# Making the second copy of v by DMA within SBUF instead of on GpSimd, in a windowed-attention and gated-layers kernel

## The chip, the cores and the metric

The kernel runs on one core of one Trainium2 chip. The metric is the device time of one execution in microseconds (us). A core has TensorE (matrix products, and weight loads beside them), VectorE (DVE in the profile), ScalarE (ACT), GpSimd (POOL) and SyncE (SP), which here does nothing but issue DMAs; 16 DMA engines move the data.

## What is computed

Three parts follow one another, all in float32:

```python
# q, k, v: (4, 8, 576, 64); a query sees itself and the 63 keys before it
scores = scale * q @ k.T                 # masked outside 0 <= i - j < 64
attn = softmax(scores)
x = (attn @ v)  reshaped to 2304 x 512
x = (silu(x @ w_gate) * (x @ w_val)) @ w_out      # 512 -> 1536 -> 512
y = ((x @ w1) * (x @ w2)) @ w3 @ w_out2           # 512 -> 1024 -> 512
```

The weights come as float64 and are read as pairs of 32-bit words.

## The kernel before

**Attention.** Two heads of one batch form a unit; there are 4 x 4 = 16 units, each cut into three sub-blocks of three 64-query windows. One iteration `m` treats two sub-blocks, so there are `NM` = 24 iterations, and the loop runs three more to drain its pipeline. In iteration `m` TensorE computes the scores of `m` (L400, L410) into PSUM, transposes raw q and k of later units (T, L373), computes the products with v of iteration `m - 3` (PV, L463) and transposes the probabilities of `m - 2` (PT, L443). VectorE takes the maxima (L417), the reciprocals of the sums (L430, L431), and evicts the transposed probabilities to SBUF (`ptt`, L449); ScalarE does the exponentials (L424) and copies the results to X (L477, L480); GpSimd multiplies the probabilities by the reciprocals (`pexp`, L434).

**The two copies of v.** A window of 64 queries needs 128 keys, that is two halves of 64. `load_v(u)` (L354, L356) loads v of unit `u` with its rows in blocks of 128. Windows that begin in the middle of a block need the halves paired the other way: the lower half of one tile from the upper part of the next block. `pair_v(u)` makes this second tile, `vt[u][1]`, by two copies on GpSimd (L362, L363), one for partitions 0 to 63 and one for 64 to 127, each 64 x 512 numbers (2 KB a partition). Units `u0` and `u0 + 1` are paired in the second and third iteration of their group of three; PV reads the copy two iterations later.

**The order.** Every engine's instructions run in the order in which the program emits them. In an iteration the loads of later units are emitted first, on SyncE: q and k (L347) four DMAs a unit, v three. `pair_v` stands behind the normalisation and ahead of `events(m, NM)`, which calls `during_attention`. There the helper work is placed: splitting the weights of the gate layer and the operands X into a high and a low part (casts L197, subtractions L201, sums L205; `narrow`, L185 to L191, turns float64 words into float32). A planner keeps a free time for each engine. `plan.charge(e, cost)` tells it what attention itself takes of an engine in this iteration; `plan.advance(3.85)` then places queued jobs on whichever of their engines can start first, as long as that start lies within the 3.85 us. Casts go to ScalarE or GpSimd, subtractions and sums to VectorE or GpSimd, the steps of `narrow` to VectorE and ScalarE alone. A job that needs a tile also needs a free slot: of 56 slots, 26 are kept for attention until it ends, and `slots` counts the others. After attention `plan.shut.add("POOL")` takes GpSimd out of the planner.

The 1 MB weight loads ("stage" loads, `st_...`, L227) go through SyncE as well. There are two buffers for them: from the third on, a stage load waits until the jobs on an earlier one are done, and SyncE issues nothing in the meantime.

**The gate.** Behind attention (and from its last three iterations on) `gated` computes the products with the weights (L578) from the split operands `xo`; from there on TensorE works without attention's interplay.

Of the kernel before, what the change touches and what calls it, by code (L numbers as in the profile page):

```python
# [32 lines left out]
def window_attention_moe_kernel(ctx: ExitStack, tc: tile.TileContext, q, k, v, w_gate, w_val, w_out, w1, w2, w3, w_out2, out):  # L33
    nc = tc.nc
# [26 lines left out]
    def slot(shape, dtype, name, counted=True):  # L61

        plan.slots -= counted
        return sl.tile(shape, dtype, tag="s", name=name)
# [266 lines left out]
    def attention(events):  # L331
        if True:
# [7 lines left out]
            raw, vt, qT, kT, sc, pexp, ptp, ptt, stat = {}, {}, {}, {}, {}, {}, {}, {}, {}  # L340
# [18 lines left out]
            def pair_v(u):  # L359

                t = slot([P, 4, 2, D], F32, f"v{u}_1", False)
                nc.gpsimd.tensor_copy(out=t[:64], in_=vt[u][0][:64, 1:])  # L362
                nc.gpsimd.tensor_copy(out=t[64:], in_=vt[u][0][64:, :4])  # L363
                vt[u].append(t)

            tbank = {}
# [146 lines left out]
            for m in range(NM + 3):  # L513
# [30 lines left out]
                for u in ((), (u0,), (u0 + 1,))[r]:  # L544
                    if u < U:
                        pair_v(u)
# [373 lines left out]
    def loads(n):  # L920
        while at[0] < min(n, len(coming)):
            coming[at[0]].load()
            at[0] += 1

    def make_to(x, rank=None):

        while at[1] <= coming.index(x):
            plan.rank = rank if rank is not None else 1 if isinstance(coming[at[1]], Weights) else 2
            loads(at[1] + 1)
            coming[at[1]].make()  # L930
            at[1] += 1
            loads(at[1] + 2)
            plan.rank = 0
# [74 lines left out]
    def during_attention(m, NM):  # L1008
        if m in (1, 3):
            loads(1 + m // 2)  # L1010
        if m == 3:
            make_to(left1[0, 1], 0)
        for tp, first in enumerate((13, 20, NM + 2)):
            if m == first:
                xop1[tp] = Operands([X[tp, c] for c in range(KC)], f"xo{tp}")
        if m < NM:
            for e, cost in (("DVE", 2.9), ("ACT", 3.2), ("POOL", 2.6)):
                plan.charge(e, cost)
            plan.advance(3.85)
        else:  # L1020
            for e, cost in (("DVE", (1.6, 1.1, 1.1)), ("ACT", (2.2, 0.5, 0.5)), ("POOL", (1.9, 0.0, 0.0))):
                plan.charge(e, cost[m - NM])
            for _ in range((3, 2, 2)[m - NM]):
                next(gate)

    with tc.manual_schedule():
        attention(during_attention)
        ident2 = own.tile([P, P], F32, name="ident2")
        nc.gpsimd.memset(ident2, 1.0)
        nc.gpsimd.affine_select(out=ident2, in_=ident2, pattern=[[-1, P]], compare_op=ALU.is_equal, fill=0.0,  # L1030
                                base=0, channel_multiplier=1)
        plan.shut.add("POOL")
        plan.slots += ATTENTION
        plan.ahead = 1.0
        for _ in gate:
            pass
        for _ in project(rows, wos, events_p):
            pass
        on(events2, len(order2) - 6, lambda: make_to(w3s[-1]))
        begin_e, run_e = final(rows2, ident2)  # L1040

        def put_all():
            for j in by:
                plan.need(j)
            begin_e()
        on(events2, len(order2) - 4, put_all)
        for _ in gated(xop2, left2, order2, AF.Copy, h2d, events2):
            pass
        run_e()
# [30 lines left out]
```

## Time and profile before

| | us |
|---|---|
| median of three runs | 873.38 |
| lowest and highest of them | 871.74, 873.64 |
| span of the profiled execution, first to last instruction | 869.7 |

The profiled execution's total is not among the times; its span is 3.7 us below the median. All times in the rows are counted from the span's start. A group of instructions reads: line, engine, operation, output<-inputs, shape, count | busy time in us, mean ns of one | idle time of the engine before them and what ended it.

### The profile page before, as it was taken

How to read it: one execution, taken by the hardware profiler on the slowest of the kernel's cores; microseconds unless marked ns; L12 is line 12 of the kernel's file. 1: busy time of each engine (PE TensorE's matmuls, PEld its weight loads, DVE VectorE, ACT ScalarE, POOL GpSimd, SP SyncE). 2: the span in 40 equal slices, each digit the busy share in tenths (PEclk: the TensorE clock that was granted, in tenths of full speed). 3: DMA queues.
4: the chain of work that ended last, by engine and by line, in shares of the span. 5: the costliest groups of instructions: out<-in, count | busy, mean ns of one | idle time of the engine just before them, and what ended most of it. 6: DMA issues, size and time to landing. Idle time of an engine off the chain costs nothing.

```text
span 869.7 us, 14819 instructions
## 1 busy us (share of the span) xinstructions
PE 839.7 (97%) x5610; PEld 791.1 (91%) x5610; DVE 582.2 (67%) x1173; ACT 421.2 (48%) x1075; POOL 86.2 (10%) x119
## 2 busy tenths in 40 slices
PE   7899888899999999999989999999999999999998
PEld 6777687899999999999989999999999998888886
DVE  4899958878688768875797573867788644531400
ACT  6878855464646454733465442445454423430300
POOL 3678930000000000000000000000000000000000
PEclk9999999999999999999999999999999999999999
DMA  9979300135356323599987331023545179131511
GB/s 198 218 159 188 93 1 37 40 126 189 111 186 219 124 104 151 200 350 402 369 300 245 119 122 49 37 71 123 194 158 193 50 267 362 39 131 64 179 49 48
DMA packets 112535, 136.23 MB, mean 157 GB/s; under 512 B 61392, under 2 KB 78032, under 8 KB 111440
## 3 DMA queue, kind: packets, MB, share of 16 engines
q1 hardware_dynamic: 112320, 135.16, 47.6%
q8 instruction: 44, 0.72, 0.4%
q14 instruction: 27, 0.22, 0.1%
q10 hardware_dynamic: 144, 0.13, 0.0%
HBM read 92.27 MB, written 42.99 MB: 156 GB/s over the span
## 4 chain that ended last, share of the span: by engine, by line
PE 81%; DVE 7%; DMA 5%; ACT 2%; SPq 2%; issue 1%; POOL 1%; POOLq 0%; ACTq 0%; DVEq 0%
PE ala L578 14%; PE alb L578 14%; PE o L707 12%; PE out L818 11%; PE beb L578 7%; PE bea L578 7%; PE acc L774 5%; PE gab L578 3%; PE gaa L578 3%; DMA wo<-wo 2%; DMA zd<-by_z 2%; PE PV L463 1%; DVE ptt L449 1%; SPq L347 1%; DMA st_z<-in_moe_w_out_dram 1%
## 5 line engine op out<-in xcount | busy, mean ns | idle before, releaser
L707 PE MATMUL o<-ph,wo 128*128 128x384 f32 x576 | 147.7, 337 | 2.7 <-ACT X L721 2.7
L707 PEld LDWEIGHTS o<-ph,wo 128*128 128x128 f32 x576 | 105.0, 189 | 3.0 <-ACT X L721 3.0
L707 PE MATMUL o<-pl,wo 128*128 128x384 f32 x288 | 96.9, 336 | 0.0
L585 ACT COPY ha<-ala 128x384 f32<-128x384 f32 x90 | 42.9, 479 | 51.5 <-PE ala L578 50.3
L589 DVE TENSOR_TENSOR ha<-ha,bea 128x384 f32<-128x384 f32 x60 | 33.2, 553 | 45.0 <-PE bea L578 26.6
L707 PEld LDWEIGHTS o<-pl,wo 128*128 128x128 f32 x288 | 54.5, 189 | 0.0
L424 ACT ACTIVATE pexp<-S,stat 128x128 f32<-128x128 f32 x144 | 51.8, 392 | 0.0
L599 ACT ACTIVATE ha<-ha 128x384 f32<-128x384 f32 x54 | 28.4, 526 | 39.0 <-DVE ha L589 39.0
L434 POOL TENSOR_TENSOR pexp<-pexp,stat 128x384 f32<-128x384 f32 x48 | 44.4, 945 | 28.5 <-DVE stat L431 22.6
L836 DVE COPY o<-out 128x512 f32<-128x512 f32 x11 | 7.6, 692 | 57.7 <-PE out L818 57.7
L201 DVE TENSOR_TENSOR pl<-pl,ph 128x768 fp32r<-128x768 f32 x36 | 33.5, 956 | 16.5 <-ACT ph L197 16.1
L197 ACT CAST ph<-pl 128x768 fp32r<-128x768 f32 x36 | 29.3, 835 | 31.1 <-DMA pl<-h 24.1
L585 ACT COPY c12b<-alb 128x384 f32<-128x384 f32 x30 | 14.5, 482 | 48.7 <-PE alb L578 48.6
L833 ACT COPY o<-out 128x512 f32<-128x512 f32 x6 | 3.5, 588 | 65.5 <-PE out L818 65.5
L589 DVE TENSOR_TENSOR c22b<-c22b,beb 128x384 f32<-128x384 f32 x30 | 16.6, 554 | 26.4 <-ACT c22b L585 26.3
L424 ACT ACTIVATION_READ_ACCUMULATOR pexp<-S,stat 128x1 f32 x144 | 33.1, 230 | 0.0
L417 DVE TENSOR_REDUCE stat<-S 128x3 f32<-128x384 f32 x48 | 24.3, 546 | 8.2 <-PE S L410 8.0
L463 PEld LDWEIGHTS PV<-ptt,v 128*64 128x64 f32 x576 | 19.5, 137 | 10.2 <-DVE ptt L449 5.7
L463 PE MATMUL PV<-ptt,v 128*64 128x64 f32 x576 | 22.9, 227 | 6.1 <-DVE ptt L449 5.0
L578 PE MATMUL ala<-xo,w_g_1h 128*128 128x384 f32 x120 | 26.9, 337 | 1.7 <-ACT w_g_1h L197 1.7
L201 DVE TENSOR_TENSOR xo<-X,xo 128x384 fp32r<-128x384 f32 x37 | 22.6, 641 | 5.7 <-ACT xo L197 5.7
L201 DVE TENSOR_TENSOR fl<-fl,fh 128x768 fp32r<-128x768 f32 x24 | 21.7, 952 | 6.9 <-ACT fh L197 6.9
(490 smaller groups left out, 2407.4 us busy)
## 6 DMA issues: line engine op xcount, KB each, us to landing
h<-ha SPq DMA_DIRECT2D x60, 384.0 KB, 3.2
pl<-h SPq DMA_DIRECT2D x36, 384.0 KB, 6.7
fl<-h SPq DMA_DIRECT2D x24, 384.0 KB, 6.1
st_w<-in_moe_w_dram SPq DMA_DIRECT2D x8, 1024.0 KB, 6.9
st_g<-in_moe_w_gate_dram SPq DMA_DIRECT2D x6, 1024.0 KB, 5.5
st_v<-in_moe_w_val_dram SPq DMA_DIRECT2D x6, 1024.0 KB, 5.4
st_wo<-in_moe_w_out_dram SPq DMA_DIRECT2D x6, 1024.0 KB, 5.8
wo<-by_wo SPq DMA_DIRECT2D x12, 512.0 KB, 3.9
```

What stands on the lines that cost most here:

```text
L197: (eng.copy if eng is nc.scalar else eng.tensor_copy)(out=hi(), in_=src())
L201: return plan.job(lambda eng: eng.tensor_tensor(out=lo(), in0=src(), in1=hi().bitcast(F32), op=ALU.subtract), after, slots=slots, DVE=dve( ...
L424: nc.scalar.activation(out=pe[:, jj, :], in_=so[:, jj, :], func=AF.Exp, bias=st[:, 0, x, jj:jj + 1], accum_out=st[:, 1, x, jj:jj + 1])
L434: nc.gpsimd.tensor_tensor(out=pe, in0=pe, in1=st[:, 3, x, :].unsqueeze(2).to_broadcast([P, SUB, P]), op=ALU.mult)
L463: nc.tensor.matmul(pp[64 * h:64 * h + 64, 64 * (SUB * x + jj):64 * (SUB * x + jj) + 64], lhsT=vt[u][e][:, at, h, :], rhs=t[:, x, jj, c:c + ...
L578: nc.tensor.matmul(acc, lhsT=self.wt.ops[p, x][:, m, :], rhs=self.xs.ops[p, m][:, y, :], start=start and n == 0, stop=n == 5, skip_group_c ...
L585: nc.scalar.copy(out=out, in_=src)
L589: nc.vector.tensor_tensor(out=out, in0=x, in1=y, op=ALU.add)
L599: nc.scalar.activation(out=h, in_=src, func=func)
L707: nc.tensor.matmul(acc[m, x], lhsT=wos.tiles[i // 6][:, i % 6, :], rhs=rows[2 * tp + x].words(f, b), start=f == n == 0, stop=f == NF - 1 a ...
L774: nc.tensor.matmul(acc, lhsT=w3T[i][c // 3][:, x, (c % 3) * P:(c % 3) * P + P], rhs=zt[c, y], start=c == n == 0, stop=c == NI - 1 and n == 2)
L818: nc.tensor.matmul(acc, lhsT=rows[blk].words(i, x)[:, t * P:t * P + P], rhs=w34[i][y], start=i == n == 0, stop=i == NI - 1 and n == 2)
```

## The change

`pair_v` issues two DMAs on SyncE, SBUF to SBUF, where it had two GpSimd copies, and GpSimd's charge for an iteration is lowered from 2.6 to 1.9 us. Nothing else changes.

```diff
             def pair_v(u):
 
                 t = slot([P, 4, 2, D], F32, f"v{u}_1", False)
-                nc.gpsimd.tensor_copy(out=t[:64], in_=vt[u][0][:64, 1:])
-                nc.gpsimd.tensor_copy(out=t[64:], in_=vt[u][0][64:, :4])
+                nc.sync.dma_start(out=t[:64], in_=vt[u][0][:64, 1:])
+                nc.sync.dma_start(out=t[64:], in_=vt[u][0][64:, :4])
                 vt[u].append(t)
...
         if m < NM:
-            for e, cost in (("DVE", 2.9), ("ACT", 3.2), ("POOL", 2.6)):
+            for e, cost in (("DVE", 2.9), ("ACT", 3.2), ("POOL", 1.9)):
                 plan.charge(e, cost)
             plan.advance(3.85)
```

## Rows read from the trace of the kernel before

**Rows 1.** The head of the page

```profile
span 869.7 us, 14819 instructions
PE 839.7 (97%) x5610; PEld 791.1 (91%) x5610; DVE 582.2 (67%) x1173; ACT 421.2 (48%) x1075; POOL 86.2 (10%) x119
```

**Rows 2.** Windows: stretch, its length, busy us of each engine (x instructions), clock, DMA

```profile
40.00:105.00 65.00, 58.07 (x968) 47.43 (x966) 60.93 (x130) 54.08 (x251) 54.71 (x71) 0.97 0.69 153
```

**Rows 3.** Waits of TensorE, 17 to 110 us: total us, times, longest

```profile
PE PV L463 <- DVE ptt L449: 4.8, 7, 1.5
PE T L373 <- DMA rawq<-in_q_dram: 1.8, 2, 1.5
PE T L373 <- DVE ptt L449: 1.4, 3, 0.6
```

**Rows 4.** Groups of VectorE, 40 to 105 us (22 two-input jobs in all)

```profile
L449 DVE COPY ptt<-PT 128x384 f32<-128x384 f32 x32 | 16.2, 544 | 0.0
...
L201 DVE TENSOR_TENSOR xo<-X,xo 128x384 fp32r<-128x384 f32 x5 | 5.7, 1151 | 0.0
...
L430 DVE TENSOR_SCALAR stat<-stat 128x6 f32<-128x6 f32 x15 | 3.0, 200 | 0.6 <-ACT pexp L424 0.6
...
L201 DVE TENSOR_TENSOR w_g_6h<-st_g,w_g_6h 128x256 fp32r<-128x256 f32 x1 | 0.4, 384 | 0.0
```

**Rows 5.** DMA, 0 to 40 us, in slices of 1 us: busy tenths, GB/s

```profile
DMA  0099999999999999936899999999999999969999
GB/s 0 14 224 219 229 220 226 214 200 186 214 203 201 211 199 208 211 73 66 301 399 357 268 213 213 213 214 220 197 328 406 336 253 209 199 124 221 227 235 211
```

**Rows 6.** Loads of v, 0 to 60 us: ns of one issue, min/median/max

```profile
L354 SPq DMA_DIRECT2D v<-in_v_dram x18: 468/542/1407, 5.3 to 49.3; - x18
```

**Rows 7.** Groups of GpSimd, whole span

```profile
L434 POOL TENSOR_TENSOR pexp<-pexp,stat 128x384 f32<-128x384 f32 x48 | 44.4, 945 | 28.5 <-DVE stat L431 22.6 <-ACT X L480 3.7 <-PE PV L463 1.4
L363 POOL COPY v<-v 64x512 f32<-64x512 f32 x16 | 10.2, 640 | 0.9
L362 POOL COPY v<-v 64x512 f32<-64x512 f32 x16 | 10.2, 636 | 0.0
```

**Rows 8.** Chain of waits, 76 to 110 us: start, us, what

```profile
103.63 1.14 POOL pexp L434
104.77 0.56 POOL v L362
...
105.38 0.62 POOL v L363
...
106.07 0.26 POOL X L205
...
107.02 1.62 POOL pexp L434 x2
```

**Rows 9.** Groups of VectorE, 160 to 200 us

```profile
L201 DVE TENSOR_TENSOR w_g_6l<-st_g,w_g_5l 128x256 fp32r<-128x256 f32 x2 | 0.8, 418 | 0.0
```

**Rows 10.** Casts to `xo`, 60 to 110 us: ns, first and last start

```profile
L197 ACT CAST xo<-X x5: 530/533/602, 66.5 to 96.0; 128x384 fp32r<-128x384 f32 x5
L197 POOL CAST xo<-X x3: 501/502/503, 68.1 to 98.7; 128x384 fp32r<-128x384 f32 x3
```

**Rows 11.** The last load of v of unit 4, issued at 29.44 us

```profile
L356 SPq DMA_DIRECT2D v<-in_v_dram x1: 607/607/607, 29.4 to 29.4; - x1
...
DMA to landing us min/median/max: 5.3/5.3/5.3
```

**Rows 12.** Timeline, TensorE, 32 to 48 us: start, us

```profile
33.22 0.92 PE L463 MATMUL PV<-ptt,v 128*64 128x64 f32 x24
...
34.07 0.87 PE L443 MATMUL PT<-ident,pexp 128*128 128x128 f32 x6
```

**Rows 13.** Timeline, VectorE, 34 to 38 us

```profile
36.49 1.01 DVE L449 COPY ptt<-PT 128x384 f32<-128x384 f32 x2
```

**Rows 14.** Waits of SyncE, 50 to 65 us

```profile
SPq L227 <- POOL w_g_3h L201: 6.8, 1, 6.8
```

## The prediction

> **What bounds the kernel now.** I read the head of the page first: a span of 869.7 us [rows 1]. The median of the three runs shown is 873.38 us, 3.7 us more; the profiled execution's own total is not given, so I make the sum against the span and carry that 3.7 us through unchanged. From about 170 us to the end TensorE is nearly always busy, and nothing that the diff touches runs there. The question is the attention stage (up to about 109 us) and the handover behind it.
>
> The windows table shows who is full there. From 40 to 105 us VectorE is busy 60.93 of 65 us and TensorE 58.07, so TensorE stands idle 65 - 58.07 = 6.9 us in that stretch, and GpSimd works 54.71 us [rows 2]. In TensorE's waits most of the idle time has one name: the attention products (PV) and the transposes (T) wait for VectorE's eviction of the transposed probabilities `ptt`, 4.8 and 1.4 us; a load is late once, for 1.8 us in two waits [rows 3]. VectorE's groups in that stretch say why: fifteen iterations (L430 x15), each with its own evictions, and between them 22 two-input jobs on lines L201 and L205 that the planner could as well have given to GpSimd, from 5 on `xo` (5.7 us) to one on `w_g_6h` (0.4 us), 20.3 us in sum [rows 4]. So VectorE sets the pace, 65 / 15 = 4.3 us an iteration.
>
> The loads are the second thing to look at. From 2 to 40 us the DMA engines are full in nearly every slice [rows 5], and SyncE issues load behind load, about 0.54 us each [rows 6]. Anything added to that queue there is added to every load behind it.
>
> **What the change removes.** 32 copies of 0.64 us on GpSimd, 10.2 + 10.2 = 20.4 us [rows 7]. GpSimd is not the pace in general, so most of this is worth only what the planner makes of it. Near the end of attention it is on the path, though: in the chain of waits both copies (0.56 and 0.62 us) stand between two normalisations of `pexp`, with one helper job behind them [rows 8]. The later normalisation can start 1.2 us earlier there, where no load is pending any more: **-1.2 us**, between 0 (something else ends that wait) and -1.2.
>
> **What the planner does with it.** GpSimd's charge falls from 2.6 to 1.9 us in 24 iterations: 16.8 us more of planned room. GpSimd's helper jobs now are 28 (119 instructions less 48 normalisations, 32 copies and 11 of set-up) in some 19 us (86.2 - 44.4 - 20.4, less set-up), 0.7 us each, so at most 16.8 / 0.7 = 24 more fit. Its window in an iteration opens at 1.9 us, before VectorE's at 2.9 and ScalarE's at 3.2, and the planner takes the earliest start; so I expect about half of the 24 to come, 12, some from ScalarE's casts and more from VectorE's 22. A job on VectorE costs 0.92 us on average there (20.3 / 22), against 0.42 us for the same kind later, when GpSimd is off [rows 4, 9]. Seven of them are 6.4 us of VectorE time. TensorE can't gain more than its idle 6.9 us. I take half of that, **-3.4 us**, because the loads below come close to their time of use and will cap it; the ends are -6.9 and +1.1 (no gain, and one pair's two issues shown once).
>
> After attention GpSimd is shut out by the code, so the handover gains only from work done earlier. That is limited by slots, not by time: 56 less 26 leave 30 counted, of which 12 hold X and 10 two weights, so 8 are left for split operands, and in fact 5 + 3 casts of `xo` run up to 99 us [rows 10]. More room on GpSimd makes no ninth: **0**, with up to -1 if the eight free their sources earlier.
>
> **What it adds.** 32 DMAs, two for each of 16 pairs of heads, on SyncE: 64 partitions by 2 KB, 128 KB each. Nothing like it (SBUF to SBUF) is in the trace. Its bounds: the stage load of 1 MB also moves 2 KB runs; while it passes, from 19 to 23 us, the four slices show 301, 399, 357 and 268 GB/s, against some 200 to 230 GB/s beside it, where the runs are 256 bytes [rows 5]. At their mean of 331 GB/s two DMAs of 131,072 bytes take 0.79 us; that is my value, since the run length is the same. The lower end is 0.66 (399 GB/s), the upper 1.08 us, two issues at 0.54 [rows 6], if issuing and not moving is what limits.
>
> Each pair also stands in SyncE's order: it waits for v to land, and the loads of q, k, v and the stage loads queue behind it. That wait itself should be short, since ten or more DMAs are issued between v and its pair. Where it bites first I find by following the queue. The pair of unit 2 stands right behind v of unit 4. That load's last DMA is issued at 29.44 and lands 5.3 us later, at 34.74 [rows 11]. With three pairs (0, 1, 2) by then, unit 2's copy lands at 34.74 + 3 x 0.79 = 37.11. The products that read it start at 33.22 [rows 12]: TensorE is 3.9 us late. But VectorE is late there already: the transposes issued at 34.07 end at 34.94 (0.87 us), and their eviction begins only at 36.49 [rows 12, 13]; 1.55 us of the delay lie beside that. So **+2.3 us** is left. The first pair also delays the stage load ahead of which it is issued by 0.79 us, but this lies inside the same delay. The ends: 0, if the queue catches up, and 1.52 + 3 x 1.08 = +4.8 with no cover. Below nothing is excluded, as the queue only gets longer. From the next pair on, the copies need no more than that lateness gives them, and the long stop of SyncE for a stage buffer (6.8 us) lets the path start afresh [rows 14].
>
> [...] No row here shows a large transfer on 64 partitions.
>
> **The sum.** 2.3 - 3.4 - 1.2 + 0 = -2.3 us: span 867.4, time 871.1 us.
>
> **The rivals.**
> *The queue becomes the pace (slower).* One mechanism, at SyncE: each pair costs its 1.08 us of issue time, so the copies and the raw loads behind them reach TensorE late and TensorE waits for DMA instead of for `ptt`. The start costs 4.8 us, the relief of VectorE is used up waiting for loads, the tail still gives 1.2: +3.6 us, 877.0 us. It decides where the relieved TensorE next waits for a load: then the -3.4 is gone, and the start costs more than the tail gives as soon as a pair takes over (1.2 + 0.03) / 3 = 0.41 us. For it: the full DMA slices and the 1.8 us already lost to a late load [rows 3, 5]. Against it: SyncE stops 6.8 us for a buffer near 54 us, which is room [rows 14]. Chance 0.27.
>
> *The room isn't used (no change).* Jobs are held by their chains (cast, then subtraction) and by slots, so few more move. Start +2.3, middle -1, tail -1.2: +0.1 us, 873.5 us. That the change doesn't do what it says belongs here: the copies go, but the time they free stays idle. Chance 0.23.
>
> *VectorE comes free (much faster).* GpSimd's copies also hold VectorE's two-input jobs up; with them gone and the queue keeping up, the whole 6.9 us of idle TensorE goes and the start's 2.3 are paid: 2.3 - 6.9 - 1.2 = -5.8 us, 867.6 us. For it: 0.92 against 0.42 us [rows 4, 9]; against it, other GpSimd jobs take the copies' place. [...] Chance 0.10.
>
> The forecast has 0.40.
>
> **How the numbers follow.** 0.2% is 1.7 us, about what a measurement of this kernel can tell from no change. Of the forecast's 0.40 I put 0.35 beyond that and 0.05 within, since -2.3 is near it; with the much faster case, faster is 0.45. Within: 0.05 and most of the unused room, 0.27. Slower: the queue and the rest, 0.28. The range reaches from just under the much faster case, 867.5, to the queue's, 877.0; left out are pairs that come late later on as well, above, and the ceilings of all terms at once, below. The likeliest case alone spans 869 to 872.
>
> **What would show it.** Right: no copies left on GpSimd; GpSimd's helper jobs up from 28 to about 40; VectorE's L201 and L205 jobs in attention fewer by about seven; TensorE's waits for `ptt` below 4 us in sum; one new wait of PV for the copy `v` of 2 to 4 us before 40 us; the first gate product 2 to 3 us earlier than now. Wrong: waits of PV or T for DMA of more than 5 us in sum (the queue), an unchanged split of the helper jobs (room not used), or a pair that takes clearly more than 1 us in the queue. If TensorE's idle time between 105 and 170 us changes by more than 2 us, the zero for the handover is wrong.

## The result, and the profile after

| | before | after |
|---|---|---|
| median, us | 873.38 | 879.85 |
| lowest and highest of 5 runs | 871.74, 875.6 | 876.87, 880.91 |
| span of the profiled execution | 869.7 | 879.2 |
| ratio after / before | | 1.008 [1.0052, 1.0109] |

The change made the kernel slower, by 6.5 us by the medians (4.5 to 9.5 by the interval). I had forecast 871.1 us, a gain. The head of the page after, the engines' shares of its chain of waits, and two groups that the change touches (columns as in [rows 1, 7]):

```profile
span 879.2 us, 14860 instructions
...
PE 843.9 (96%) x5610; PEld 793.8 (90%) x5610; DVE 579.9 (66%) x1168; ACT 421.6 (48%) x1075; POOL 70.1 (8%) x92
...
PE 77%; DMA 9%; SPq 6%; DVE 4%; ACT 2%; issue 1%; ACTq 0%; DVEq 0%
...
L434 POOL TENSOR_TENSOR pexp<-pexp,stat 128x384 f32<-128x384 f32 x48 | 43.5, 928 | 53.9 <-DVE stat L431 36.8
...
L463 PE MATMUL PV<-ptt,v 128*64 128x64 f32 x576 | 25.7, 236 | 7.1 <-DMA v<-v 5.1
```

and the shares of the chain before:

```profile
PE 81%; DVE 7%; DMA 5%; ACT 2%; SPq 2%; issue 1%; POOL 1%; POOLq 0%; ACTq 0%; DVEq 0%
```

GpSimd is relieved as meant: 70.1 us busy against 86.2, and it waits 53.9 us ahead of its normalisations against 28.5 [rows 1, 7]. But SyncE's queue (SPq) and the DMAs now hold 15% of the chain instead of 7%, and the products with v wait for a new thing, `v<-v`, the copy. All of TensorE's waits in the attention stage, 17 to 115 us (columns as in [rows 3]):

```profile
PE T L373 <- DMA rawq<-in_q_dram: 6.3, 3, 2.9
PE PV L463 <- DMA v<-v: 5.1, 8, 1.0
PE T L373 <- DVE ptt L449: 2.0, 3, 1.2
PE PV L463 <- DVE ptt L449: 1.3, 2, 0.8
```

Before, `ptt` cost these two 6.2 us and loads 1.8 [rows 3]; other waits came to 2.1. Now `ptt` costs 3.3 and loads (the copies counted with them) 11.4. So TensorE now waits mainly for loads where it waited for VectorE, and longer. That VectorE itself was relieved doesn't follow from this; the experiments come back to it.

SyncE's timeline after, around the first two pairs (start, us, instruction), says why. Each line begins within 0.1 us of the end of the one before it: the queue has no gap.

```profile
17.54 0.60 SPq L362 DMA_DIRECT2D v<-v  x1
18.18 0.82 SPq L363 DMA_DIRECT2D v<-v  x1
19.05 0.59 SPq L227 DMA_DIRECT2D st_g<-in_moe_w_gate_dram  x1
19.68 1.12 SPq L347 DMA_DIRECT2D rawq<-in_q_dram  x2
20.85 2.73 SPq L347 DMA_DIRECT2D rawk<-in_k_dram  x2
23.62 0.99 SPq L362 DMA_DIRECT2D v<-v  x1
24.65 0.59 SPq L363 DMA_DIRECT2D v<-v  x1
25.29 1.17 SPq L347 DMA_DIRECT2D rawq<-in_q_dram  x2
```

The first pair holds the queue for 1.5 us (17.54 to 19.05), the second for 1.7 (23.62 to 25.29). TensorE's timeline after, with the idle time before an instruction in brackets, shows where that arrives:

```profile
26.18 0.88 PE L373 MATMUL T<-ident,rawq 96*128 96x96 f32 x6 [2.68 <-DMA rawq<-in_q_dram]
...
28.68 0.48 PE L463 MATMUL PV<-ptt,v 128*64 128x64 f32 x4 [0.35 <-DMA v<-v]
29.09 1.54 PE L443 MATMUL PT<-ident,pexp 128*128 128x128 f32 x6
...
37.63 0.45 PE L463 MATMUL PV<-ptt,v 128*64 128x64 f32 x8
38.79 0.69 PE L463 MATMUL PV<-ptt,v 128*64 128x64 f32 x16 [0.70 <-DMA v<-v]
...
69.53 0.69 PE L373 MATMUL T<-ident,rawq 96*128 96x96 f32 x6 [2.86 <-DMA rawq<-in_q_dram]
...
71.89 0.48 PE L463 MATMUL PV<-ptt,v 128*64 128x64 f32 x4 [0.94 <-DMA v<-v]
72.30 1.54 PE L443 MATMUL PT<-ident,pexp 128*128 128x128 f32 x6
```

First TensorE waits 2.68 us for raw q, which SyncE issued at 19.68, behind the first pair; it starts on it at 26.18, where before it waited 1.54 us and started at 24.25. Then it waits for the copies themselves. The 24 products that started together at 33.22 before [rows 12] come in two parts: eight at 37.63, and the sixteen behind the wait for the copy at 38.79, 5.6 us after the start of the group before. The stall repeats at 69.5 us. Twice the transposes of the probabilities take 1.54 us where the same six took 0.87 [rows 12]: after these waits the granted clock was lower, 0.66 and 0.54 on average over two stretches that show 1.00 before. The windows of TensorE (stretch, its length, PE busy, granted clock, DMA share, GB/s) after:

```profile
24.00:34.00 10.00, 7.47 (x73) 0.66 1.13 219
71.00:82.00 11.00, 10.11 (x102) 0.54 1.05 202
```

and before, in the same stretches:

```profile
24.00:34.00 10.00, 9.09 (x160) 1.00 1.24 259
71.00:82.00 11.00, 9.56 (x161) 1.00 0.90 190
```

From 71 to 82 us TensorE is busier than before and gets through 102 recorded matmuls instead of 161.

To follow the loss I marked when TensorE began the scores of some iterations and the first gate product, read from its timeline in the profiled execution of each kernel:

| us | scores of 5 | of 7 | of 15 | first gate product | ratio to before |
|---|---|---|---|---|---|
| before | 26.3 | 34.7 | 69.1 | 109.0 | |
| after | 30.3 | 40.0 | 80.2 | 119.2 | 1.008 |

+4.0, +5.3, +11.1, +10.2. Behind the first gate product nothing is lost: from there to the end it is 760.7 us before and 760.0 after. The profiled executions differ by 9.5 us, more than the medians: after's took 880.91 us, 1.7 more than its span and 1.1 more than its median, and with as much beside its span before's took 871.4, 2.0 less than its median. One wait of TensorE for `ACT X L721` in the projection, far from the change, takes between 1.0 and 3.1 us in the traces of before, after, e1 and e14 and is part of that scatter.

### The profile page after: what moved, and what is told of

Its sections match the earlier page's. It is cut to its first block, busy times and chain, and to the rows that moved or that the text cites. A ratio compares the mean times of both kernels' runs of the same rounds, so it can differ in the third digit from the quotient of the medians.

```text
span 879.2 us, 14860 instructions
## 1 busy us (share of the span) xinstructions
PE 843.9 (96%) x5610; PEld 793.8 (90%) x5610; DVE 579.9 (66%) x1168; ACT 421.6 (48%) x1075; POOL 70.1 (8%) x92
## 4 chain that ended last, share of the span: by engine, by line
PE 77%; DMA 9%; SPq 6%; DVE 4%; ACT 2%; issue 1%; ACTq 0%; DVEq 0%
PE ala L578 14%; PE alb L578 13%; PE o L707 11%; PE out L818 11%; PE bea L578 6%; PE beb L578 6%; PE acc L774 5%; PE gaa L578 3%; PE gab L578 3%; SPq L347 2%; DMA wo<-wo 2%; SPq L354 2%; DMA zd<-by_z 2%; DMA v<-v 1%; DMA st_g<-in_moe_w_gate_dram 1%
## 5 line engine op out<-in xcount | busy, mean ns | idle before, releaser
L585 ACT COPY ha<-ala 128x384 f32<-128x384 f32 x90 | 42.7, 478 | 53.3 <-PE ala L578 52.0
L589 DVE TENSOR_TENSOR ha<-ha,bea 128x384 f32<-128x384 f32 x60 | 33.2, 553 | 46.1 <-PE bea L578 27.4
L434 POOL TENSOR_TENSOR pexp<-pexp,stat 128x384 f32<-128x384 f32 x48 | 43.5, 928 | 53.9 <-DVE stat L431 36.8
L599 ACT ACTIVATE ha<-ha 128x384 f32<-128x384 f32 x54 | 28.3, 526 | 39.0 <-DVE ha L589 38.9
L197 ACT CAST ph<-pl 128x768 fp32r<-128x768 f32 x36 | 29.3, 836 | 29.6 <-DMA pl<-h 22.5
L589 DVE TENSOR_TENSOR c22b<-c22b,beb 128x384 f32<-128x384 f32 x30 | 16.6, 554 | 26.3 <-ACT c22b L585 26.2
L424 ACT ACTIVATION_READ_ACCUMULATOR pexp<-S,stat 128x1 f32 x144 | 33.2, 230 | 0.0
L463 PE MATMUL PV<-ptt,v 128*64 128x64 f32 x576 | 25.7, 236 | 7.1 <-DMA v<-v 5.1
L463 PEld LDWEIGHTS PV<-ptt,v 128*64 128x64 f32 x576 | 21.3, 145 | 11.8 <-issue 4.0
L417 DVE TENSOR_REDUCE stat<-S 128x3 f32<-128x384 f32 x48 | 24.4, 548 | 11.2 <-PE S L410 11.1
L449 DVE COPY ptt<-PT 128x384 f32<-128x384 f32 x48 | 24.6, 548 | 6.5 <-PE PT L443 6.3
```

The lines of the kernel that those rows point to most:

```text
L197: (eng.copy if eng is nc.scalar else eng.tensor_copy)(out=hi(), in_=src())
L424: nc.scalar.activation(out=pe[:, jj, :], in_=so[:, jj, :], func=AF.Exp, bias=st[:, 0, x, jj:jj + 1], accum_out=st[:, 1, x, jj:jj + 1])
L434: nc.gpsimd.tensor_tensor(out=pe, in0=pe, in1=st[:, 3, x, :].unsqueeze(2).to_broadcast([P, SUB, P]), op=ALU.mult)
L463: nc.tensor.matmul(pp[64 * h:64 * h + 64, 64 * (SUB * x + jj):64 * (SUB * x + jj) + 64], lhsT=vt[u][e][:, at, h, :], rhs=t[:, x, jj, c:c + ...
L585: nc.scalar.copy(out=out, in_=src)
L589: nc.vector.tensor_tensor(out=out, in0=x, in1=y, op=ALU.add)
```

## The experiments

The times below are (ratio - 1) times the median of before on the same chip (870.85 us for e1 to e4, 871.06 for e5 to e8, 870.49 for e9 to e12, 872.25 for e13 to e15). The table gives the marks of all of them; the text says what they mean. A mark is read from one execution: that of e1 took 3.9 us less than the median of its kernel, that of e7 3.8 less and that of e10 4.4 more, and from the first gate product to the end the traces take from 757 to 763 us. So differences of a few us between marks prove little, and the ratios decide.

| us | scores of 5 | of 7 | of 15 | first gate product | ratio [95%] |
|---|---|---|---|---|---|
| e1 DMA, old charge | 30.6 | 39.7 | 74.8 | 114.6 | 1.0073 [1.005, 1.0096] |
| e2 charge alone | - | - | - | - | 1.0014 [0.9995, 1.0034] |
| e3 stage loads held | 30.0 | 40.1 | 75.5 | 118.5 | 1.0074 [1.0046, 1.0102] |
| e4 ScalarE's queue | 29.6 | 46.0 | 82.8 | 122.8 | 1.017 [1.0146, 1.0194] |
| e5 TensorE kept busy | 29.7 | 39.7 | 76.8 | 115.4 | 1.0078 [1.0049, 1.0107] |
| e6 from unit 4 on | 25.9 | 34.3 | 70.0 | 109.7 | 1.0017 [0.9999, 1.0036] |
| e7 four DMAs a pair | 30.5 | 43.6 | 84.9 | 129.0 | 1.0232 [1.0205, 1.0258] |
| e8 last two units | 27.0 | 35.2 | 68.9 | 107.6 | 1.0006 [0.9987, 1.0026] |
| e9 a quarter of the bytes | 29.8 | 38.9 | 71.7 | 110.8 | 1.0025 [1.0002, 1.0047] |
| e10 GpSimd's queue | 31.6 | 42.7 | 75.5 | 119.8 | 1.0106 [1.0072, 1.014] |
| e11 from unit 4 on, new charge | 27.1 | 35.0 | 71.9 | 111.2 | 1.0042 [1.0023, 1.0061] |
| e12 charge alone | 26.1 | 34.3 | 68.5 | 111.9 | 1.0032 [1.0013, 1.0051] |
| e13 charge alone, loads held | 26.1 | 34.5 | 66.1 | 110.0 | 1.0021 [1.0001, 1.0041] |
| e14 the change again | 29.8 | 39.8 | 79.9 | 118.9 | 1.0061 [1.004, 1.0083] |
| e15 first four units | 30.2 | 39.8 | 73.3 | 112.7 | 1.0038 [1.0021, 1.0055] |

**Which half of the change costs?** My first theory after the result had two costs: the DMAs in SyncE's queue, and the lower charge. With more planned room the planner emits the third stage load earlier, so that at 62.3 us it goes out ahead of raw q of a later unit instead of behind it; I held that for the stall at 69.5 us. Its rival: the DMAs alone. First the DMAs with the old charge, then the charge with the old copies:

```diff
-            for e, cost in (("DVE", 2.9), ("ACT", 3.2), ("POOL", 1.9)):
+            for e, cost in (("DVE", 2.9), ("ACT", 3.2), ("POOL", 2.6)):
```

> The copies go by DMA on SyncE as in the change, but GpSimd's charge stays 2.6, so the planner's placement and the place of the third and fourth stage loads in SyncE's order are those of before. Theory A (two costs: the copies delay the loads behind them at the start, and the lower charge moves stage loads ahead of the raw loads of units 10 and 14): the first cost alone is left, attention 4 to 5 us late at iteration 7 and no second step at iterations 14 and 15; 875 to 877 us. Theory B (the copies in SyncE's order cost time all along, the charge is irrelevant): 879 to 881 us, the second step of about 6 us at iterations 14 and 15 is still there.

```diff
 # before, copies on GpSimd
-            for e, cost in (("DVE", 2.9), ("ACT", 3.2), ("POOL", 2.6)):
+            for e, cost in (("DVE", 2.9), ("ACT", 3.2), ("POOL", 1.9)):
```

> The copies stay on GpSimd, only the charge falls from 2.6 to 1.9. Theory A: the stage loads move as in the change, the transposes of units 10 and 14 wait for raw q and k; iteration 14 starts 4 to 6 us later against before, with nothing lost at the start; 876 to 879 us. Theory B: no DMA is added, so no loss: 871 to 874 us.

e1 loses 6.4 us, as much as the whole change; e2 loses 1.2 us [-0.4, +3.0]. (e2 has no marks; e12 below is the same kernel.) The stall near 70 us is indeed smaller in e1's trace, whose scores of 15 come at 74.8 instead of 80.2, yet by the ratios that doesn't shorten the whole. In e3 the charge stays new and stage loads are kept out of the iterations in question:

```diff
+        (plan.shut.add if 4 <= m <= 10 or 12 <= m <= 18 else plan.shut.discard)("SP")
         if m < NM:
```

> The change with its charge of 1.9, but the planner may not issue stage loads in iterations 4 to 10 and 12 to 18, so the third and fourth stand in SyncE's order where they stand before. Theory A: the step at iterations 14 and 15 is gone, the start's 4 to 5 us stay, and VectorE's relief may give a little back; 874 to 877 us. Theory B: 879 to 881 us.

e3 loses 6.4 us too. Its scores of 15 come at 75.5, so the stall near 70 us is smaller there as well. But one iteration takes 7.5 us later on (from 98.1 to 105.6), and the first gate product comes at 118.5, near the change's 119.2. No load stands in the chain of waits there: a cast of `xo` on GpSimd (99.96), its subtraction on VectorE (100.44) and the eviction `ptt` behind it (101.77) do, which is what the lower charge brings about, as shown further down. So the theory that the stage loads' new place is the second cost fell.

**Is it SyncE's queue?** With the old charge, e4 issues the DMAs on ScalarE, and e10 (run later) on GpSimd:

```diff
-                nc.sync.dma_start(out=t[:64], in_=vt[u][0][:64, 1:])
-                nc.sync.dma_start(out=t[64:], in_=vt[u][0][64:, :4])
+                nc.scalar.dma_start(out=t[:64], in_=vt[u][0][:64, 1:])    # e10: nc.gpsimd
+                nc.scalar.dma_start(out=t[64:], in_=vt[u][0][64:, :4])    # e10: nc.gpsimd
```

> The copies go by DMA, issued by ScalarE, with the charge of 2.6: the same bytes, but not in SyncE's order, and SyncE issues nothing more than before. If SyncE's issuing and order are the start's cost, it goes (below 2 us at iteration 7) unless ScalarE's own issuing (32 x about 0.5 us) takes its place: 872 to 875 us. If it is the DMA engines' time, the start's lateness stays at 3 us or more: 875 to 878 us.

> The copies go by DMA issued by GpSimd, charge 2.6: the bytes are the same, SyncE issues nothing more, and GpSimd issues where it copied before. If SyncE's queue is the cause: TensorE's waits for raw q as before (2 to 3 us), the total between 2 us below and 2 us above before, unless issuing holds GpSimd up for more than the 0.64 us of a copy. If the DMA engines' time is the cause: 4 us or more above before.

Both lose more: 14.8 and 9.2 us, which by the expectations spoke for the DMA engines' time. But TensorE's waits for raw q fall to 0.3 and 0.5 us (2.8 in e1), so that part did belong to SyncE's queue; what comes in its place is that an issue stands in its engine's order. ScalarE's timeline in e4 shows it idle for 5.15 us, the two issues of a pair going out at 29.91 and 32.54 within that time, and the copy of q right behind the second (the profile puts the end of the wait down to a load of k):

```profile
29.91 0.48 ACTq L362 DMA_DIRECT2D v<-v  x1
32.54 0.47 ACTq L363 DMA_DIRECT2D v<-v  x1
33.06 0.71 ACT L385 ACTIVATE qT<-T 128x288 f32<-128x288 f32 x2 [5.15 <-DMA rawk<-in_k_dram]
```

On GpSimd the issue of a copy takes nearly as long as making it did (tile `v` on GpSimd, e10: count, ns of one, min/median/max, first and last start), against 0.64 us for the copy [rows 7], and the products then wait 8.3 us for the landing:

```profile
L362 POOL DMA_DIRECT2D v<-v x16: 555/561/701, 16.6 to 119.4; - x16
L363 POOL DMA_DIRECT2D v<-v x16: 516/516/522, 17.3 to 120.0; - x16
```

**Issuing, bytes or the clock?** e7 moves the same bytes with four issues a pair, e9 has the two issues but moves one block of four (the products read that block; three quarters of the copied bytes are left out), and e5 gives TensorE eight products with nothing to wait for in iteration 4, to see whether its granted clock then stays up. All have the old charge, so they stand against e1.

```diff
+                for p in (0, 32):                                       # e7
+                    nc.sync.dma_start(out=t[p:p + 32], in_=vt[u][0][p:p + 32, 1:])
+                for p in (64, 96):
+                    nc.sync.dma_start(out=t[p:p + 32], in_=vt[u][0][p:p + 32, :4])
...
+                nc.sync.dma_start(out=t[:64, :1], in_=vt[u][0][:64, 1:2])   # e9
+                nc.sync.dma_start(out=t[64:, :1], in_=vt[u][0][64:, :1])
...
+                        e, at = (1, 0) if j % 2 == 0 and j else (0, j // 2)
...
+                if m == 4:                                              # e5
+                    fill = bank("fill")[:, :SUB * P]
+                    for _ in range(8):
+                        nc.tensor.matmul(fill, lhsT=identr, rhs=mask[0], start=True, stop=True)
```

> Each copy by two DMAs of 32 partitions: the same bytes, four issues a pair instead of two; charge 2.6. If issuing on SyncE is the cost of a pair, the start's lateness about doubles (8 us or more at iteration 7) and the total is 4 to 7 us above the two-issue kernel. If the moving of the bytes is, the total is within 2 us of it.

> As the DMA copies with the old charge, but each DMA moves one of the four blocks (512 bytes a partition, a quarter of the bytes), and PV reads that block where it would read another: part of v's pairing is left out. The issues and their order are unchanged. If issuing and SyncE's order cost the time: within 1.5 us of the full copies, that is 4.5 to 7 us above before, iteration 7 still 4 us late. If moving the bytes does: the loss falls to a quarter, 1 to 3 us above before.

> The DMA copies with the old charge, and eight more products of 128x384 (about 0.3 us each, 2.4 us together) in iteration 4, between the scores and the transposes that wait for raw q of unit 4, so that TensorE is not idle there. Their result is not used. Theory C (what turns 2 to 3 us of waiting into 5 is the clock: after that wait the granted clock is 0.50 from 26 to 32 us): the granted clock stays at 1.00 between 26 and 34 us, iteration 7 is 2 to 3 us late instead of 5, total 2 to 3 us below the same kernel without them. Theory D (the lateness comes from the queue alone): iteration 7 is 5 us late or more, and the total is the same within 1 us.

e7 loses 20.2 us, 13.8 more than e1 where I had expected 4 to 7. Its scores of 7 come 8.9 us later than before's. The start as I had written it is 1.52 us plus three pairs; with a pair at four issues of 0.6 us that makes 1.52 + 3 x 2.4 = 8.7. SyncE's timeline of e7 shows one pair, four issues, 3.1 us:

```profile
23.73 1.88 SPq L363 DMA_DIRECT2D v<-v  x2
25.65 1.22 SPq L365 DMA_DIRECT2D v<-v  x2
```

while the DMA engines are less full than in e1 (share 0.94 against 1.15, 236 GB/s against 253, from 20 to 30 us). With a quarter of the bytes, e9 issues as slowly as e1: two issues of a pair take 1.14 us by the medians (1.12 in e1), and raw q behind the second pair goes out at the same time. SyncE's timelines of e9 and of e1:

```profile
24.50 2.26 SPq L347 DMA_DIRECT2D rawq<-in_q_dram  x2
...
24.53 1.93 SPq L347 DMA_DIRECT2D rawq<-in_q_dram  x2
```

TensorE's waits from 17 to 115 us agree: for raw q 2.9 us in e9 and 2.8 in e1, for the copies 3.4 and 5.5. The scores of 7 are still 4.2 us late (5.0 in e1). So at the start the number of issues sets most of the delay. The whole is another matter: e9 loses 2.2 us [0.2, 4.1], what I had expected if moving the bytes costs, against e1's 6.4 [4.4, 8.4]. So the bytes count in how much of the delay is made up later; by which path wasn't followed further.

In e5 the granted clock was 1.00 from 26 to 28 us, where e1 has 0.50, but behind the next wait for a copy, which ends at 28.26 us, it was lower all the same (windows of TensorE in e5, columns as above):

```profile
26.00:28.00 2.00, 0.88 (x22) 1.00 1.21 214
28.00:30.00 2.00, 1.74 (x11) 0.61 1.31 213
30.00:32.00 2.00, 2.00 (x27) 0.53 0.80 126
```

The scores of 7 come at 39.7 us as in e1, and the whole loses 6.8 us. So the clock of 1.00 in that stretch gained nothing: TensorE reached its wait for a copy earlier and waited longer there, 1.38 us against 0.92 in e1. The same for the stretch from 71 us wasn't tried.

**Where along the stage?** e6 makes the DMA only for units 4 to 15, e15 only for 0 to 3, both with the old charge; e8 only for units 14 and 15, the tail of my forecast. The others are copied on GpSimd.

```diff
+                if u >= 4:              # e15: u < 4; e8: u >= 14
                     nc.sync.dma_start(out=t[:64], in_=vt[u][0][:64, 1:])
                     nc.sync.dma_start(out=t[64:], in_=vt[u][0][64:, :4])
+                else:
+                    nc.gpsimd.tensor_copy(out=t[:64], in_=vt[u][0][:64, 1:])
+                    nc.gpsimd.tensor_copy(out=t[64:], in_=vt[u][0][64:, :4])
```

> The copies of units 0 to 3 stay on GpSimd, those of units 4 to 15 go by DMA on SyncE; charge 2.6. If the start is where the time goes, iterations up to 8 start as before and the total is within 2 us of before (869 to 873 where before has 871). If the queue costs all along, 3 to 5 us remain.

> Only the copies of units 0 to 3 by DMA, units 4 to 15 on GpSimd, charge 2.6. If the start is where the time goes: iteration 7 about 5 us late as with all sixteen, and 3.5 to 5.5 us above before in the end. If the lateness of the start is caught up later: below 2 us above before, and the loss of all sixteen needs the later ones too.

> Only the copies of units 14 and 15 go by DMA, where no load is pending any more; charge 2.6. If the last normalisations wait for GpSimd's copies as the chain of before says, 1.2 us less than before; if something else ends that wait, the same within 0.5 us.

Four pairs cost 3.3 us [1.8, 4.8], the other twelve 1.5 [-0.1, 3.1]; together 4.8, against e1's 6.4 [4.4, 8.4]. So about half of the loss, by the medians, comes from the first four pairs, when SyncE has no gap. e8 shows neither gain nor loss, +0.5 us [-1.1, +2.3]. The copies are gone from its chain of waits near the end, but VectorE's evictions and maxima stand in their place, with nothing of GpSimd in the chain from 95 to 118 us.

**What does the lower charge do?** e11 is e6 with the new charge, e12 repeats e2, e13 is e2 with the stage loads held as in e3.

> Units 0 to 3 copied on GpSimd, units 4 to 15 by DMA on SyncE, and the charge 1.9. The predicted relief of VectorE (3.4 us) has its best chance here. If it exists, the total is 2 us or more below the same kernel with the charge of 2.6, that is below before; if the loads take it, the same within 1.5 us of that kernel, 0 to 3 us above before.

> The copies on GpSimd with the charge of 1.9 once more, for its trace: the transposes of units 10 and 14 wait longer for raw q than before if the stage loads ahead of them matter, 2 to 4 us each; in the first run the total was 1.2 us above before, between 0.4 below and 3.0 above, so a part of that must be given back elsewhere.

> The copies on GpSimd and the charge 1.9, with the third and fourth stage loads held at their old places in SyncE's order. The charge alone measured 1.2 and 2.8 us above before. If the stage loads that it moves ahead of the raw loads of units 10 and 14 are what costs, this one is at before or below it (-1.5 to +1 us). If it is GpSimd's fuller order (more helper jobs between the normalisations), 1.5 to 3 us above before remain.

It costs rather than gains: e11 3.7 us [2.0, 5.3] against e6's 1.5, e12 2.8 [1.1, 4.4], e13 1.8 [0.1, 3.6], beside e2's 1.2. In e12 the waits for raw q are 3.3 us in sum and 1.6 at the longest, less than the 2 to 4 us each that I had expected if the stage loads mattered. The chain of waits of e12 has the place (start, us, what):

```profile
92.33 0.83 POOL pexp L434
93.15 0.56 POOL v L362
...
93.76 0.62 POOL v L363
...
94.44 0.51 POOL xo L197
...
94.97 1.34 DVE xo L201
96.31 0.48 DVE ptt L449
...
96.83 1.21 PE PV L463 x24
```

The planner, told that GpSimd has room, puts a cast of `xo` there and its subtraction on VectorE. In GpSimd's order the cast stands behind a normalisation and both copies; VectorE, also in order, waits for it, and the eviction `ptt` that TensorE needs stands behind the subtraction. VectorE's wait, 60 to 112 us of e12:

```profile
DVE xo L201 <- POOL xo L197: 4.2, 2, 3.6
```

e13 has the same wait of 3.6 us with the stage loads held back, so this wait is GpSimd's fuller order and not the loads. The scores right behind it, of 21, fall back by 3.5 and 3.6 us against before in e12 and e13. The change itself has a smaller wait, 2.3 us.

VectorE has fewer helper jobs in e12, 17 from 40 to 112 us where before has 22, and yet TensorE's waits for `ptt` grow there, from 6.2 to 8.3 us for these two (17 to 110 us):

```profile
PE PV L463 <- DVE ptt L449: 4.7, 4, 3.2
PE T L373 <- DVE ptt L449: 3.6, 4, 1.3
```

In e1, where VectorE has 23, the same two come to 2.8 us. So the short waits for `ptt` come with the DMAs and not with fewer jobs on VectorE.

**The change again**, beside e13 and e15 on one chip, to see whether the charge's loss adds to that of the DMAs:

> The change itself beside the others on one chip. With the old charge the DMA copies measured 6.4 us above before (ratio 1.0073). If the charge's own loss adds to it, 8 to 10 us above before; if it is lost in the waiting for loads, 5 to 7.5 us.

It loses 5.3 us, and its scores of 15 come late as in the first run (79.9 against 80.2). That's not more than e1's 6.4 (the intervals overlap, [3.5, 7.2] and [4.4, 8.4]), so nothing shows that the two losses add. That a late VectorE costs nothing more where TensorE waits for loads would explain it, but no run shows that.

No version beat the kernel before; e8 and e6 come nearest to it. Issuing the pairs later in SyncE's order, behind the loads that TensorE needs first, wasn't tried.

## Why the prediction was wrong

**The step that failed: the price of a pair in the start.** I wrote that two DMAs of 128 KB take 0.79 us "since the run length is the same", and kept two issues as the upper end "if issuing and not moving is what limits". In the start issuing is what limits. Tile `v` after, on SyncE (ns of one, min/median/max), 0 to 115 us:

```profile
L362 SPq DMA_DIRECT2D v<-v x16: 467/603/2397, 17.5 to 111.3; - x16
L363 SPq DMA_DIRECT2D v<-v x16: 588/595/1526, 18.2 to 112.4; - x16
```

A pair is 1.2 us of SyncE's time by the medians, and more where issues are drawn out, as in the timeline above. 1.52 + 3 x 1.2 = 5.1 us, and the scores of 7 came 5.0 to 5.3 us later in after, e1, e14 and e15. Moving wasn't mis-sized, as far as one pair tells. Unit 2's pair, issued right behind the v of unit 4 (same view, one instruction at a time, with its time to landing):

```profile
L356 SPq DMA_DIRECT2D v<-in_v_dram x1: 775/775/775, 32.4 to 32.4; - x1
...
DMA to landing us min/median/max: 5.4/5.4/5.4
...
L362 SPq DMA_DIRECT2D v<-v x1: 602/602/602, 33.2 to 33.2; - x1
...
DMA to landing us min/median/max: 5.0/5.0/5.0
...
L363 SPq DMA_DIRECT2D v<-v x1: 595/595/595, 33.9 to 33.9; - x1
...
DMA to landing us min/median/max: 4.8/4.8/4.8
```

The v lands at 32.4 + 5.4 = 37.8 us, 3.0 us later than before [rows 11], put back by the two pairs ahead; the pair itself lands at 33.9 + 4.8 = 38.7, 0.9 us behind it, near my 0.79 (in e9, with a quarter of the bytes, 0.55). So the start is 1.52 + 3.0 + 0.9 = 5.4 us: I had priced all three pairs by what they move, and the two ahead cost the queue's time. What one of the two DMAs takes to move by itself isn't shown: issued at 33.2 and 33.9, both overlap with that load, which lands at 37.8.

**The cover of 1.55 us hardly helped.** I let part of the delay lie beside a late eviction on VectorE. The eviction was late, but TensorE had other work in the meantime: before, it waited only 0.25 us ahead of the products that need it (at 37.18). After, the eviction is 4.4 us later (40.89 against 36.49 [rows 13]) and the scores of 8 are 5.3 us late all the same, like those of 7. The long stop of SyncE for a stage buffer (6.8 us) [rows 14], which was to let the path start afresh, shrank to 0.3 us (17 to 70 us): the lateness had used up that room. What did hold is that a pair waits little for its own v: 0.7 us of SyncE's waits after, from 17 to 115 us (in e1 the last pair waits 4.4 us, with nothing behind it).

PV was not the first to suffer either. I followed the queue to unit 2's copy and took the delay behind the first pair to lie inside the same lateness; raw q, issued behind that pair, stopped TensorE at 26.2 us already, and 4.0 of the 5.3 us were lost by the scores of 5.

**The middle, -3.4 us.** GpSimd's helper jobs rose from 28 to 33 (92 instructions less 48 normalisations and 11 of set-up), not to 40. VectorE's fell from 22 to 19, not to 15 (40 to 112 us). The waits for `ptt` fell from 6.2 to 3.3 us, below the 4 us I had named, but not for the reason I gave: they fall as well with the DMAs and the old charge (2.8 in e1), and they grow with the charge alone (8.3 in e12). No run shows a gain from fewer jobs on VectorE; the charge by itself measured 1.2 to 2.8 us of loss. I had counted what the planner may place, and not that a job placed on an in-order engine holds up the engine that waits for its result, as the cast on GpSimd held up VectorE for 3.6 us in e12. Nor did VectorE come free as in the last rival: with the copies gone its two-input jobs take 0.96 us on average (18.3 / 19) where they took 0.92, and the groups of 128x256 among them 0.79 to 1.03 us, by their means, against the later 0.42 [rows 9]. So no run shows that GpSimd's copies held those jobs up.

**The tail, -1.2 us,** isn't shown: e8 measured +0.5, and its interval from -1.1 to +2.3 just leaves it out. VectorE takes over the chain there. **The handover, 0,** was right: from the first gate product to the start of the projection it is 278 us before and after.

**Term by term,** then: the start took 5.3 us by the scores of 7 where I had 2.3, the middle gave nothing or a loss where I had -3.4, the tail +0.5 where I had -1.2, and the later pairs, which I had at nothing, 1.5 [-0.1, 3.1] by e6.

**The rival was right in its mechanism.** "The queue becomes the pace" named SyncE, the issue time, and TensorE waiting for DMA instead of `ptt`, as it came; so did the sign that I had set, over 5 us of waits for DMA (11.4). It gave 877.0 us. Its start, 4.8, was near the 5.3 measured; it still credited the tail with 1.2 us, and it took the loss to end with the start, where e6 suggests that the later pairs add some (its interval just takes in none).

## What to carry to other kernels

Price a DMA that is added to a full issue queue by the time its issuer needs for it (here 1.2 us a pair by the medians, where I had put 0.79), and charge that to every load behind it; the bytes counted beside it, in how much is made up later (a loss of 2.2 us was left with a quarter of them, of 6.4). Look first at the units for which the queue has no gap: here the first four pairs cost 3.3 us, the twelve behind them 1.5. And lowering what a planner believes an engine to be charged with moves other jobs into that engine's order, so try it by itself: here it measured 1.2, 2.8 and 1.8 us of loss without any DMA.

## What the runs showed of the hardware

In after the granted clock was lower behind waits of TensorE for loads, of 2.7 us ahead of 26.2 and of 2.9 and 0.9 us ahead of 69.5 and 71.9: 0.66 on average from 24 to 34 us and 0.54 from 71 to 82, and six transposes took 1.54 us instead of 0.87. The kernel before shows the same behind a wait of 1.5 us for `ptt` that ends at 46.68: 0.50 from 48 to 50 us, and 1.54 us for six transposes; but behind its wait of 1.5 us for raw q that ends at 24.25 it shows 1.00 from 24 to 34 us. So the work behind some of these waits took longer too, 0.67 us more for six transposes, though in e5 a clock of 1.00 up to 28 us left the scores of 7 at 39.7 us as in e1. An issue of a 64-partition DMA within SBUF took, by the medians of the first and second of a pair, 0.60 and 0.60 us on SyncE (after), 0.47 and 0.58 on ScalarE (e4) and 0.56 and 0.52 on GpSimd (e10), and with a quarter of the bytes 0.55 and 0.60 on SyncE (e9; 0.53 and 0.60 in e1). GpSimd issued a pair in 1.08 us where copying it took 1.28, so handing the copies to DMAs that it issued itself saved it 0.2 us a pair.
